# SyncE's queue asks for batch 1's q, k and v behind small reads of w_ch1's landed quarters

## Chip, cores and metric

The kernel runs on one core of one Trainium2 chip. The metric is the device time of one execution in microseconds (us). The profile's times count from the start of its span.

## The reference

Four batches, eight heads, 768 positions, head dimension 64. Attention with a window of 128 positions and 4 sink positions is followed by a residual MLP that mixes positions and then channels:

```python
scores = scale * q @ k^T             # kept where pos_k < 4 or 0 <= pos_q - pos_k < 128
x   = softmax(scores) @ v            # heads joined: (batch, 768, 512)
a1  = alpha1 * x + beta1
tok = einsum('ts,bsd->btd', w_tok, a1)
u   = x + lam * tok
a2  = alpha2 * u + beta2
out = u + lam * (relu(a2 @ w_ch1) @ w_ch2)     # w_ch1 512x2048, w_ch2 2048x512
```

Everything is given and returned in float32; the kernel multiplies in float16.

## The kernel before

One batch goes through these stages; the names are those of tiles in the profile.

- **Loads.** `nat` holds q or k of two heads (128x2x384 float32, 384 KB); a batch has eight of them, named by head pair and by q or k (`nat_1_0` is q of head pair 1). `load_qk` (L481) asks for them on SyncE's queue, but for six of batch 0 that GpSimd loads with a cast. `load_v` (L500) asks for `vnat`, six per batch, 256 KB each. `load_w` (L537) asks for `wst`, a staging tile with a pair of row blocks of w_ch2 (512 KB, eight in all). `load_w1` (L542) asks on GpSimd's queue, with a cast to float16, for `w1f`, a resident tile, in four quarters of 512 columns (512 KB each as written).
- **Transposes.** q and k are cast to `n` and turned by TensorE (`tp`, batches 0 and 1) or by DMA (batches 2 and 3) into `qkT`. The rows of w_tok are loaded to `wtn`, cast to `wt` and turned (`wT`) into `wtokT`.
- **Attention.** `S` holds scores, `sk` those of the sinks, `E` their exponentials, `pv` the products with v (cast to `vfs`), `x` the normalized result. VectorE normalizes (`rec` and `x`, L817 and L818), GpSimd multiplies by lam times alpha1 (`xh`), and VectorE adds the beta part (L841).
- **MLP.** `tok` multiplies `wtokT` with six `xh` tiles (six matmuls for each of six row tiles). VectorE adds it to `x`, `u` is the float16 copy, `uTp` its transposes in PSUM, `uT` the result of the affine step (two chunks of three row tiles each). `h` is the hidden layer: a unit is four matmuls for a chunk and one of 16 column blocks `fi` of w_ch1, and `h_0_5` is chunk 0, `fi` 5; it needs quarter `fi // 4` of `w1f`. Its relu is `hT`. `ch` multiplies it with `w2f`, which is w_ch2 times `lam_b`, made from `wst` by VectorE or GpSimd (L898), two products per `wst` tile.

The order on each engine is not written by hand. Every step is a task with a priority, a cost per engine and the tasks it needs; `Plan.run` (L130) plays the tasks through in advance and emits them in the order in which they then start. `Rings` (L35) models the two DMA queues there. `TURNS` is a list of seeds; each seed moves some priorities a little before the plan is made (`shuffle`, L262). Where TensorE would idle in the plan ahead of 36 us, matmuls on a zero tile are put in (`idle`, L342).

Buffers come in numbered homes: 8 for `nat`, 4 for `wst`, 4 for `vnat`, 12 for `x`, and 4 PSUM buffers `d` that `pv`, `tok`, `h`, `ch` and most transposes share. Two of the `wst` homes hold v of batch 0's second head group at first. An engine waits in its order: what stands behind a waiting instruction waits too. In the emitted program each DMA of SyncE's queue has one of eight semaphores in turn and waits for the transfer that had it before.

The tasks for the loads of batch 1 need nothing in the kernel before:

```python
for i, (hp, t) in enumerate(QK_ORDER):
    load_qk(t0 + 100 + i, 1, hp, t)
...
for r in range(NR):
    load_v(t0 + 300 + r, 1, r)
```

Of the kernel before, what the change touches and what calls it, by code (L numbers as in the profile page):

```python
# [10 lines left out]
FP16 = mybir.dt.float16  # L11
# [4 lines left out]
PE, ACT, DVE, POOL, SP = "pe", "act", "dve", "pool", "sp"  # L16
# [13 lines left out]


FW = 1.0


class Rings:  # L35
# [74 lines left out]
class Plan:  # L110
# [9 lines left out]
    def add(self, prio, engs, fn, after=(), uses=(), mode=None, lands=None, port=False,  # L120
            since=0.0):


        t = Task(len(self.tasks), prio, engs, fn, after, uses, mode, lands, port, since)
        for a in t.needs:
            a.then.append(t)
        self.tasks.append(t)
        return t

    def run(self, prio):  # L130
# [17 lines left out]
        rings = Rings()  # L148
# [3 lines left out]
        def end(t, seen):  # L152
            t.seen = seen
            for b in t.uses:
                b.left -= 1
                b.freed = max(b.freed, seen)
                if b.left == 0:
                    busy[b.kind][b.home] = False
                    homes[b.kind][b.home] = b.freed
            for o in t.then:  # L160
                ready[o.i] = max(ready[o.i], seen)
                waiting[o.i] -= 1
                if not waiting[o.i]:
                    bisect.insort(open_, (rank[o.i], o.i))
# [33 lines left out]
        while len(steps) < len(tasks):  # L198
            best = pick()
            if best is None or landing <= best[0]:  # L200
                assert landing < float("inf"), "no task can go on"
                t = rings.step(float("inf"))
                end(t, rings.now + 300.0)
                landing = rings.peek()
                continue
            start, r, _, i, e = best
            open_.pop(bisect.bisect_left(open_, (r, i)))
            t = tasks[i]
            for b in t.uses:
                if b.home is None:  # L210
                    b.home = min((h, n) for n, (h, x) in enumerate(zip(homes[b.kind], busy[b.kind]))
                                 if not x)[1]
                    busy[b.kind][b.home] = True
            idle = None
            n = int((start - max(free[PE], 400.0)) / (took if free[PE] > 4500.0 else 110.0))
            if e == PE and free[PE] < until and n > 0:
                spare = [(h, k) for k, (h, x) in enumerate(zip(homes["d"], busy["d"])) if not x]
                if spare and min(spare)[0] <= free[PE]:
                    idle = (min(spare)[1], n)
                    homes["d"][idle[0]] = start  # L220
                    mode = None
            cost = t.engs[e]
            if t.lands:
                cost += rings.room("sw" if e == POOL else "hw", t.lands, start) - start
            if e == PE:
                if start < 4500.0:
                    cost = cost * 2
                if t.mode != mode:
                    cost = cost + 95
                mode = t.mode  # L230
            free[e] = start + cost
            if e == POOL or (e == DVE and t.port):
                port = free[e]
            steps.append((t, e, start, free[e], idle))
            if t.lands:
                rings.step(start)
                rings.issue("sw" if e == POOL else "hw", t, free[e])
                landing = rings.peek()
            else:
                end(t, free[e] + SEEN[e])  # L240
# [34 lines left out]
def kernel(  # L275
# [123 lines left out]
    w1f = const.tile([P, NC, DFF], FP16, name="w1f")  # L399
    w2f = const.tile([P, NF, DM], FP16, name="w2f")  # L400

    ROWS = 7000.0

    PAIRS = 0

    TURNS = (39286, 39315, 39323, 39754, 40467, 41250, 41382, 139002, 39003, 39015, 139040, 139062, 139089, 139154, 39159, 139160, 39171, 39387, 139559, 139625, 139757, 139905, 39966, 140019, 140036, 140073)
    W1_SINCE = 20000.0

    V0 = (((0, 1), (2, 3), (4, 5)), ((0, 1, 2), (3, 4, 5)))
# [7 lines left out]
    done = {}  # L417
# [82 lines left out]
    def load_v(p, b, r, wait=None):  # L500
        bf = vn[b, r] = Buf("vnat", None, None, f"vnat{b}_{r}")
        done["vn", b, r] = add(
            p, {SP: 550}, lambda e: nc.sync.dma_start(
                bf.t, v[b, :, r * P : (r + 1) * P, :].rearrange("h p d -> p h d")),
            [wait], [bf], lands=(64, 19.0))
# [31 lines left out]
    def load_w(p, key, src):  # L537
        bf = wst[key] = Buf("wst", None, None, f"wst_{key}")
        done["wst", key] = add(
            p, {SP: 400}, lambda e: nc.sync.dma_start(bf.t, src), uses=[bf], lands=(16, 90))  # L540

    def load_w1(p, i):  # L542
        done["w1", i] = add(
            p, {POOL: 760}, lambda e: nc.gpsimd.dma_start(
                w1f[:, :, i * 512 : (i + 1) * 512],
                moe_w_ch1[:, i * 512 : (i + 1) * 512].rearrange("(c p) f -> p c f", p=P)),
            lands=(32, 96), since=W1_SINCE)

    def load_w2(p, i):
        for a in range(4 * i, 4 * i + 4, 2):  # L550
# [541 lines left out]
    load_w1(-770, 0)  # L1092
    for i in range(1, 4):
        load_w1(-769, i)

    def fold_rows():
        for name, key, o, p in (("a1", "la1", la1_b, -987), ("b1", "lb1b", lb1_b, -986)):
# [36 lines left out]
    for b in range(B):  # L1134
        w0 = STEP * b
        if b == 0:
            seq = [("tok", ti) for ti in range(3)] + [("uT", 0, 0), ("uT", 0, 1)]
            seq += [("tok", ti) for ti in range(3, NR)]
            m1 = []
            for qd in range(4):  # L1140
                for chk in range(2):
                    m1 += [("m1", chk, fi) for fi in range(4 * qd, 4 * qd + 4)]
            m1.insert(3, ("uT", 1, 0))
            m1.insert(5, ("uT", 1, 1))
        else:
            seq = [("tok", ti) for ti in range(NR)]
            m1 = [("m1", 0, fi) for fi in range(NF)]
            m1 += [("m1", 1, fi) for fi in range(NF)]
        seq += m1
        seq += [("m2", ti, part) for ti in range(NR) for part in range(4)]  # L1150
        ns = len(seq)
        if b == 0:
            for i, (hp, t) in enumerate(QK_ORDER):
                load_qk(t0 + 100 + i, 1, hp, t)
            done["lam"] = add(
                t0 + 150, {SP: 500}, lambda e: nc.sync.dma_start(
                    lam_b, moe_lam.unsqueeze(0).to_broadcast([P, DM])), lands=(8, 90))
            for i in range(4):
                load_w2(t0 + 200 + i, i)
                cast_w2(w0 + 22 + 4 * i, i)  # L1160
            for r in range(NR):
                load_v(t0 + 300 + r, 1, r)
        for i, (what, *args) in enumerate(seq):

            p = w0 + i - (LEAD if b and what == "tok" and args[0] < 3 else 0)
            {"tok": tok, "uT": uTp, "m1": mlp1, "m2": mlp2}[what](p, b, *args)
            if b and what == "tok":
                uTx(p + 0.3, b, *args)
        if b + 1 < B:
            nb = b + 1  # L1170
            if nb >= XB:
                for i, (hp, t) in enumerate(QK_ORDER):
                    load_qk(w0 + i, nb, hp, t, done["qkT", b, 3, 1])
                for r in range(NR):
                    load_v(w0 + 10 + r, nb, r, done["qkT", b, 3, 1])
            lo, hi = (1, ns - 14) if b else (LO, ns - 12)
            steps = [("T", i) for i in range(8)] + [("sk",)]
            for j in range(NR):
                steps += [("S", j)]
                steps += [("pv", j - 1, 0), ("pv", j - 1, 1)] if j else [("vs",)]  # L1180
            steps += [("pv", NR - 1, 0), ("pv", NR - 1, 1)]
            for r in range(NR):
                cast_v(w0 + lo + (hi - lo) * (r + 4) / len(steps), nb, r)
            for i, (what, *args) in enumerate(steps):
                p = w0 + lo + (hi - lo) * i / len(steps) + 0.5
                if what == "T":
                    hp, t = QK_ORDER[args[0]]
                    trans(p if nb < XB else w0 - 15 + i, nb, hp, t, {POOL: 829, ACT: 831}, {DVE: 955, ACT: 800},
                          wait=done["tok", b, 2])
                elif what == "sk":  # L1190
                    sinks(p, nb)
                elif what == "vs":
                    fill_vs(p, nb)
                elif what == "S":
                    j = args[0]
                    scores(p, nb, j, (0, 1) if j < NR - 1 else (None,))
                else:
                    pv(p, nb, *args)
# [37 lines left out]
```

The softmax here doesn't subtract the row's maximum and nothing guards it: scores larger than these inputs give would overflow.

## Time and profile before

| | |
|---|---|
| median of 6 runs | 262.83 us (262.21 to 263.61) |
| profiled execution, its own time | 263.61 us |
| its span | 261.9 us |
| TensorE matmul busy | 253.5 us, 97% |
| VectorE busy | 155.9 us, 60% |
| ScalarE busy | 134.2 us, 51% |
| GpSimd busy | 81.0 us, 31% |
| TensorE clock granted | full in all 40 slices |
| SyncE's DMA queue | 35.14 MB, 56.2% of 16 DMA engines |
| GpSimd's DMA queue | 3.28 MB, 7.7% |

The profiled execution is the slowest of the six. Busy time is the time in which an engine has an instruction in it; issuing of DMAs is not counted. SP is SyncE, PE is TensorE, DVE is VectorE, ACT is ScalarE and POOL is GpSimd.

### The profile page before, as it was taken

The page shows a single profiled execution, that of the slowest core. Times are in us where ns is not written, and L with a number is a line of the kernel's source. Part 1 is how long each engine was busy: PE and PEld are TensorE (multiplying, and loading weights), DVE is VectorE, ACT ScalarE, POOL GpSimd, SP SyncE. Part 2 cuts the span into 40 slices and gives each one's busy share as a digit, 9 for nine tenths or more (in the row PEclk, how much of TensorE's full clock was granted, in tenths as well). Part 3 has the DMA queues.
Part 4 walks back from the last instruction along what each step waited for, and adds up shares of the span by engine and source line. Part 5 has one row for each costly group of instructions (what it writes and reads, how often), then busy time and mean ns, then how long its engine had stood idle before and what let it go on. Part 6 is the DMA issues. An engine that isn't in the chain of part 4 may idle for free.

```text
span 261.9 us, 4960 instructions
## 1 busy us (share of the span) xinstructions
PE 253.5 (97%) x1954; PEld 139.8 (53%) x1954; DVE 155.9 (60%) x315; ACT 134.2 (51%) x219; POOL 81.0 (31%) x100
## 2 busy tenths in 40 slices
PE   7899989899999999999999999999999999999994
PEld 7554646465555544565555445556555445655453
DVE  4697994779999936755668534459965444000222
ACT  2788667479882224767741126788411136773000
POOL 8539951454711612143427203004223000000000
PEclk9999999999999999999999999999999999999999
DMA  7999999959936998899917669400012233000222
GB/s 177 195 244 373 297 290 279 299 132 316 216 82 168 238 200 186 176 219 217 174 50 170 167 128 228 84 0 3 0 41 83 68 92 83 0 0 3 81 80 80
DMA packets 85791, 38.76 MB, mean 148 GB/s; under 512 B 73460, under 2 KB 79868, under 8 KB 85768
## 3 DMA queue, kind: packets, MB, share of 16 engines
q1 hardware_dynamic: 81984, 35.14, 56.2%
q0 software_dynamic: 3744, 3.28, 7.7%
q8 instruction: 15, 0.25, 0.4%
q14 instruction: 8, 0.07, 0.1%
q10 hardware_dynamic: 40, 0.03, 0.0%
HBM read 29.91 MB, written 6.29 MB: 138 GB/s over the span
## 4 chain that ended last, share of the span: by engine, by line
PE 82%; DMA 11%; POOL 3%; DVE 2%; issue 0%; POOLq 0%
PE ch L1052 31%; PE h L996 28%; PE tok L916 9%; DMA w1f<-in_moe_w_ch_dram 7%; PE pv L792 4%; PE S L702 4%; DMA n<-in_k_dram 4%; PE S L697 1%; PE ch L1023 1%; POOL n L486 1%; POOL xh L827 1%; PE pv L785 1%; DVE x L841 1%; DVE E L731 1%; PE sk L639 1%; DVE x L818 0%
## 5 line engine op out<-in xcount | busy, mean ns | idle before, releaser
L996 PE MATMUL h<-uT,w1f 128*128 128x384 f16 x512 | 89.2, 326 | 1.5 <-DMA w1f<-in_moe_w_ch_dram 1.0
L1052 PE MATMUL ch<-w2f,hT 128*128 128x512 f16 x368 | 86.5, 379 | 0.1
L996 PEld LDWEIGHTS <-w1f 128*128 128x128 f16 x512 | 48.2, 98 | 34.8 <-issue 3.3
L1002 ACT ACTIVATE hT<-h 128x384 f16<-128x384 f32 x103 | 50.2, 491 | 25.2 <-PE h L996 24.6
L1052 PEld LDWEIGHTS <-hT 128*128 128x128 f16 x368 | 34.4, 98 | 38.1 <-issue 1.0
L722 ACT ACTIVATE E<-S 128x1024 f16<-128x1024 f32 (+1 forms) x42 | 40.6, 1003 | 12.2 <-PE S L702 10.6
L834 POOL TENSOR_TENSOR xh<-x,la_b 128x512 f16<-128x512 f32 x18 | 25.5, 1424 | 52.0 <-DVE x L818 36.2
L1063 DVE TENSOR_TENSOR x<-x,ch 128x512 f32<-128x512 f32 x23 | 15.8, 686 | 35.4 <-PE ch L1052 35.3
L916 PE MATMUL tok<-xh,wtokT 128*128 128x512 f16 x144 | 33.7, 379 | 0.0
L349 ACT CAST u<-x 128x512 f16<-128x512 f32 x17 | 10.5, 618 | 42.5 <-DVE x L923 42.5
L923 DVE TENSOR_TENSOR x<-x,tok 128x512 f32<-128x512 f32 x24 | 16.3, 686 | 19.8 <-PE tok L916 19.7
L841 DVE SCALAR_TENSOR_TENSOR x<-lb_b,rsum,x 128x512 f32<-128x512 f32 x24 | 22.1, 932 | 5.2 <-POOL xh L834 4.9
L1004 DVE TENSOR_SCALAR hT<-h 128x384 f16<-128x384 f32 x25 | 13.9, 555 | 16.6 <-PE h L996 16.2
L916 PEld LDWEIGHTS <-wtokT 128*128 128x128 f16 x144 | 14.0, 98 | 16.3
L818 DVE TENSOR_TENSOR x<-pv,rec 128x256 f32<-128x256 f32 x48 | 20.4, 425 | 1.7
L351 POOL CAST vfs<-vnat 128x512 f16<-128x512 f32 x18 | 12.7, 710 | 20.5 <-DMA vnat<-in_v_dram 12.9
L792 PEld LDWEIGHTS <-E 128*128 128x128 f16 x328 | 15.1, 97 | 6.4 <-issue 0.6
L731 DVE TENSOR_TENSOR E<-E,maskn 128x1024 f16<-128x1024 f16 x25 | 18.1, 745 | 0.0
L792 PE MATMUL pv<-vfs,E 128*128 128x65 f16 x328 | 17.8, 194 | 0.0
L351 POOL CAST u<-x 128x512 f16<-128x512 f32 x7 | 5.2, 742 | 37.1 <-DVE x L923 37.1
L351 POOL CAST n<-nat 128x768 f16<-128x768 f32 x12 | 10.1, 850 | 16.2 <-DMA nat<-in_q_dram 7.9
L349 ACT CAST n<-nat 128x768 f16<-128x768 f32 x12 | 9.9, 832 | 8.1 <-DMA nat<-in_k_dram 7.3
(99 smaller groups left out, 207.9 us busy)
## 6 DMA issues: line engine op xcount, KB each, us to landing
out_dram<-x SPq DMA_DIRECT2D x23, 256.0 KB, 2.4
nat<-in_q_dram SPq DMA_DIRECT2D x13, 384.0 KB, 5.4
nat<-in_k_dram SPq DMA_DIRECT2D x13, 384.0 KB, 7.2
vnat<-in_v_dram SPq DMA_DIRECT2D x18, 256.0 KB, 4.5
wst_w<-in_moe_w_ch_dram SPq DMA_DIRECT2D x8, 512.0 KB, 11.5
wtn<-in_moe_w_tok_dram SPq DMA_DIRECT2D x6, 384.0 KB, 5.5
w1f<-in_moe_w_ch_dram POOLq DMA_DIRECT2D x4, 512.0 KB, 15.6
v<-in_v_dram SPq DMA_DIRECT2D x12, 128.0 KB, 6.6
```

Of the source, the lines that this page charges most:

```text
L349: nc.scalar.copy(o, i)
L351: engine[e].tensor_copy(o, i)
L722: nc.scalar.activation(eT.t, pS.t[:, :, 0 : n * w].rearrange("p e (i w) -> p e i w", i=n), AF.Exp, scale=scale)
L731: nc.vector.tensor_mul(ev, ev, m.to_broadcast(list(ev.shape)))
L792: nc.tensor.matmul(po.t[:, hl, :], eT.t[:, e_, off + i, c : c + P], vf[j][:, h, :], start=(r < 2 and n == 0), stop=(n == len(parts) - 1 an ...
L818: nc.vector.tensor_mul(bx.t[:, 4 * G : 4 * G + 4, :], po.t[:, :, 0:D], rec.t.to_broadcast([P, 4, D]))
L834: engine[e].tensor_mul(bh.t, bx.t.rearrange("p h d -> p (h d)"), la1_b)
L841: engine[e].scalar_tensor_tensor(out=xf, in0=lb1_b, scalar=rsum[:, r : r + 1], in1=xf, op0=ALU.mult, op1=ALU.add)
L916: nc.tensor.matmul(pt.t, wtokT[:, si, ti * P : (ti + 1) * P], hs[si].t, start=(si == 0), stop=(si == NR - 1))
L996: nc.tensor.matmul(ph.t, w1f[:, c, fi * P : (fi + 1) * P], bu.t[:, c, chk * NTOK : (chk + 1) * NTOK], start=(c == 0), stop=(c == NC - 1))
L1002: nc.scalar.activation(bh.t[:, fi, :], ph.t, AF.Relu)
L1052: nc.tensor.matmul(pc.t, bh.t[:, fi, nt * P : (nt + 1) * P], w2f[:, fi, :], start=(fi == 0), stop=(fi == NF - 1))
```

## The change

A small tile `gates` is added. `gate(i)` is a DMA on SyncE's queue that reads eight elements of quarter `i` of `w1f` in SBUF into `gates`; as it reads the quarter, the program makes it wait for the quarter's landing. `GATES = (-1, 2, 3)` sets which landing the tasks of three groups of loads wait for in the plan: w_ch2's none, batch 1's q and k that of quarter 2, batch 1's v that of quarter 3. The plan now takes a GpSimd transfer for landed 1800 ns after its last byte in the model instead of 300 (`SWDONE`). The list `TURNS` is another one, so the order of all engines differs through the whole program; SyncE's order is given in the prediction as far as it matters.

```diff
+SWDONE = 1800.0
...
-                end(t, rings.now + 300.0)
+                end(t, rings.now + (SWDONE if POOL in t.engs else 300.0))
...
+    gates = const.tile([1, 32], FP16, name="gates")
+
+    GATES = (-1, 2, 3)
...
-    TURNS = (39286, 39315, 39323, ... 26 seeds)
+    TURNS = (176180, 41742, 158411, ... 21 seeds)
...
     def load_w(p, key, src):
-            p, {SP: 400}, lambda e: nc.sync.dma_start(bf.t, src), uses=[bf], lands=(16, 90))
+            p, {SP: 400}, lambda e: nc.sync.dma_start(bf.t, src), [done.get(("w1", GATES[0]))], uses=[bf], lands=(16, 90))
...
+    def gate(i):
+
+        add(-3000, {SP: 420}, lambda e: nc.sync.dma_start(
+            gates[0:1, 8 * i : 8 * i + 8], w1f[0:1, 0, i * 512 : i * 512 + 8]), [done["w1", i]],
+            lands=(1, 20))
...
+    for i in sorted(set(GATES)):
+        if i < 0:
+            continue
+        gate(i)
...
-                load_qk(t0 + 100 + i, 1, hp, t)
+                load_qk(t0 + 100 + i, 1, hp, t, done.get(("w1", GATES[1])))
...
-                load_v(t0 + 300 + r, 1, r)
+                load_v(t0 + 300 + r, 1, r, done.get(("w1", GATES[2])))
```

## The prediction

> **What bounds the kernel now.** I read the busy shares first, then windows cut at the places where TensorE stops, then its order of time, the chain of waits and SyncE's queue.
>
> ```profile
> PE 253.5 (97%) x1954; PEld 139.8 (53%) x1954; DVE 155.9 (60%) x315; ACT 134.2 (51%) x219; POOL 81.0 (31%) x100
> ```
> TensorE is the bound. The windows (length, then busy time per engine; clock, DMA share and GB/s at the end) say where it is not full:
>
> ```profile
> 34.82:38.48 3.66, 2.67 (x38) 2.15 (x37) 3.56 (x6) 3.44 (x5) 2.67 (x4) 1.00 1.12 293
> 38.48:50.70 12.22, 10.90 (x76) 6.29 (x77) 7.05 (x13) 7.63 (x15) 3.02 (x5) 1.00 1.13 296
> 50.70:60.00 9.30, 9.30 (x74) 5.81 (x76) 7.20 (x12) 6.51 (x14) 6.61 (x7) 1.00 0.65 158
> 60.00:92.00 32.00, 32.00 (x270) 17.29 (x267) 29.98 (x56) 19.31 (x27) 12.67 (x10) 1.00 0.88 205
> 92.00:258.60 166.60, 166.51 (x1110) 88.64 (x1108) 80.88 (x158) 75.69 (x130) 31.68 (x34) 1.00 0.47 100
> ```
> From 50.70 to the end nothing is left to win; only the stretch before it has holes. TensorE's order of time there:
>
> ```profile
> 34.82 1.69 PE L597 MATMUL tp<-iden,n 128*128 128x128 f16 x18
> 37.16 0.84 PE L957 MATMUL uTp<-iden,u 128*128 128x128 f16 x12 [0.64 <-POOL u L351]
> 39.11 1.46 PE L996 MATMUL h<-uT,w1f 128*128 128x384 f16 x7 [0.32 <-DVE uT L942]
> 46.95 2.75 PE L916 MATMUL tok<-xh,wtokT 128*128 128x512 f16 x12
> 50.70 0.50 PE L996 MATMUL h<-uT,w1f 128*128 128x384 f16 x2 [1.00 <-DMA w1f<-in_moe_w_ch_dram]
> ```
> Per group of the chain of waits TensorE needs 0.65 us for four h matmuls (one "unit"), 1.29 for six tok, 0.34 for six transposes. Between 34.82 and 50.70 stand 6 groups of transposes of batch 1 (2.0), 2 of uTp (0.7), 2 of wT (0.7), 10 h units (6.5) and 12 tok matmuls (2.6): 12.45 us of work in 15.88, so **3.4 us are lost**, 1.96 of them as bracketed waits. The last is for a quarter of w1f:
>
> ```profile
> 31.04 19.62 DMA w1f<-in_moe_w_ch_dram
> 50.70 2.12 PE h L996 x12
> ```
> The four quarters, issued by GpSimd at 23.42, 24.23, 28.84 and 31.04, land 10.6, 15.4, 15.7 and 19.6 us later: about 34.0, 39.6, 44.5 and 50.7, over 5 us apart. In that time SyncE's queue is full:
>
> ```profile
> 30.03 1.65 SPq L1156 DMA_DIRECT2D lam_b<-in_moe_lam_dram  x1
> 32.57 5.36 SPq L540 DMA_DIRECT2D wst_w<-in_moe_w_ch_dram  x3
> 39.13 9.40 SPq L503 DMA_DIRECT2D vnat<-in_v_dram  x2
> ```
> Two issues take 9.4 us because, in the program's list, every SyncE transfer waits for the landing of the one eight places earlier.
>
> **What the Trainium skill says.** "DMA: Bandwidth & Descriptors", section "Queues, rings and completion order": each DMA engine goes round-robin over the rows that have work, packet by packet. So w1f's row gets more when SyncE's is empty. The trace agrees as far as it goes: 5 us per 512 KB quarter with both rows full at 293 to 296 GB/s. The same page, "Anatomy of one DMA — SWDGE (gpsimd) path": a semaphore wait is served on the issuing sequencer. So a read that waits for a quarter holds all behind it in SyncE's order; the 9.4 us above show such holding. "Perfetto Trace Analysis", "Tensor Engine Instruction (MATMUL, LD_WEIGHTS)": the end of a matmul is estimated. Agreed: 18 transposes show 1.69 us "busy" for 1.01 of work, so I count starts, not busy time.
>
> **The change, part by part.** Both instruction lists side by side show three things.
>
> (a) SyncE's order. Before, eight q and k loads of batch 1 (384 KB each) stand between and behind the w_tok loads, issued 19.3 to 29.3. After, it is: v and w_tok of batch 0, seven of the eight w2 loads and lam, gate 2, eight q/k, the last w2, gate 3, six v. 3.1 MB of q and k and 0.5 MB of v leave the stretch in which w1f travels; its w2 loads come earlier. Till w1f is complete there are then from 21 us: 1.6 MB w_tok, 2.1 w2, 0.26 lam, 2.1 w1f, 6.1 MB in all, at 290 GB/s 21 us: the last quarter by about 42, not 50.7; the third by 40. Bounds: 37 (the 373 GB/s of the best slice) and 50 (no gain).
>
> (b) TensorE's order. Work is the same but for 97 fillers for 88, nine of 0.065: 0.6 us, all but one ahead of tok. All six tok run before h; h begins with quarter 0; batch 1's transposes move behind h_0_8, h_1_7 and h_0_9 (quarter 2). Before, 207.9 us pass from h_0_0 (50.70) to the last matmul (258.62). After, the 6 groups of transposes and 10 units that before stand ahead of h_0_0 stand behind it: 2.0 + 6.5. So **the end = start of h_0_0 + 216.4**, if nothing stalls later; equal time at 42.2.
>
> When does h_0_0 start? VectorE's order now puts the casts wt_0, wt_1, wt_2 ahead of x_4 and of the second head group. wt_0 waits for the first w_tok landing: 16.58 + 5.2 = 21.8 before, one place earlier now, say 21.3. Then wt 3 x 0.87, six normalizations x 0.55, vs 0.34 and one wtokT copy 0.5 give x_3 at 28.1; GpSimd's xh of it (0.7) ends between 28.8 and, behind the earlier ones, 29.7. I take tok_0 at 29.3 (29.24 before), with five wT done instead of three. From tok_0 to h_0_0 lie 36 tok x 0.2157, one wT, two uTp: 8.8 us. But VectorE still has two x, three wtokT, five beta steps (0.74 to 1.02) and the adds (0.62) to do; u_2 is cast by 38.0 to 38.4 and TensorE is at uTp by 37.5: 0.5 to 0.9 lost. After uTp the four affine steps (0.67 on ScalarE, 0.43 on VectorE) have no transposes of batch 1 to cover them any more: 1.3. h_0_0 at 29.3 + 8.8 + 2.3 = 40.4, so the end at 256.8: **1.8 us less**.
>
> (c) The gates. Two issues of 0.4 us on SyncE's queue, hidden. The trace shows no such tiny transfer; landing between 1.7 us (the shortest of all, a 128 KB output) and the page's fixed cost of about 2; only the transfer eight places on waits for it: nothing. The wait itself: the w2 load ahead of gate 2 needs a staging buffer that VectorE frees with w2_2's second product, behind h_0_2's relu, about 43.6. So gate 2 is reached at 44.1, after quarter 2: wait 0, at worst 0.4 beyond a landing at 44.5. Behind it wait the eight loads: issued from 44.5, first landed at 48 to 49 (4 us, the shortest of their kind), then 1.2 us each (384 KB at 300), eighth by 57; GpSimd's casts 0.85 each, done at 58. TensorE asks for the first at 52.8 (18 units and two uTp after 40.4), for the last at 60.3 (seven more groups with seven units between, 0.99 each, and a unit extra): cover of 2.3 us. The v loads land from 60 on, first wanted at 63.5. If that cover is gone, each further us of delay costs one us.
>
> (d) The planner's SWDONE and new TURNS only change the order of the later batches; at tok, h and ch of batches 1 to 3 both lists keep the same distances within 1 us, so I take 0, with -0.3 and +0.8 as ends.
>
> Sum: -1.8 against the profiled execution (span 261.9, last matmul 258.62, own time 263.61; median of six 262.83). From the median: **261.0**.
>
> **Rivals.** *Early chain eats it*: if w_tok lands 1 to 2 us later than 21.3, or the four PSUM buffers hold pv behind x_4, tok_0 moves one for one and h_0_0 comes at 41.4 to 42.9: 262.0 to 263.5. For it: VectorE is 12.95 of 15 us busy in 14 to 29. Against: in the order before it also waits till 22.6 for its first wt. *Larger gain*: the affine and uTp holes are half as large and tok_0 comes at 28.3 since five wT are done: 259.0. *Loads too late (slower)*: SyncE's order makes q/k wait for gate 2 and for VectorE's w2 products. With the eighth cast at 58 for 60.3, it begins to cost when the loads begin at 46.8, it outweighs the gain of 1.8 beyond 48.6, and at 51 it gives 265.2. TensorE's order is fixed, so nothing else slips in between. For it: VectorE's 5 w2 products took 4.58 us beside GpSimd, 0.92 each instead of 0.69. Against: 2.3 us of cover. *The gates do nothing*: the queue reaches them after the landings and the move is all in the order; the time is the forecast's.
>
> **How the numbers follow.** Forecast with the larger gain 0.63; early chain 0.18 (mostly within the bound); loads too late or a stall in the later batches 0.19. A measurement tells about 0.3%, 0.8 us, from no change: faster below 262.0, slower above 263.6. The likeliest alone spans 259.0 to 262.0; the range to 264.2 takes in the early chain and half of the late loads.
>
> **What would show it.** Right: w1f's landings 10 to 13 us after issue, the last by 43; no wait of TensorE for w1f; SyncE at gate 2 at 43 to 45; holes only around uTp, 2 us; h_0_0 at 40 to 41 and solid after. Wrong: h_0_0 after 42.2; a wait of tp or of its cast on nat; holes after 62.

## The result, and the profile after

| | before | changed |
|---|---|---|
| median | 263.14 us (262.21 to 264.35, 73 runs) | 264.32 us (262.46 to 266.59, 36 runs) |
| ratio to before | | 1.0044 (95%: 1.0032 to 1.0055) |
| profiled execution, its own time | 263.61 us | 263.59 us |
| its span | 261.9 us | 261.9 us |

The change makes the kernel slower by 0.44%, 1.2 us. The forecast was 261.0, faster. The two profiled executions are alike in time, which hides that most executions of the changed kernel (26 of 36) are slower than this one; they spread over 4 us where the old ones spread over 2.

First TensorE's order of time after the change (start, length, engine, line, what, shape, count, and in brackets the wait ahead of it):

```profile
29.53 1.03 PE L927 MATMUL tok<-xh,wtokT 128*128 128x512 f16 x4
...
31.65 6.32 PE L927 MATMUL tok<-xh,wtokT 128*128 128x512 f16 x28
38.04 0.27 PE L968 MATMUL uTp<-iden,u 128*128 128x128 f16 x2
38.70 0.73 PE L968 MATMUL uTp<-iden,u 128*128 128x128 f16 x10 [0.38 <-ACT u L351]
40.05 0.32 PE L1007 MATMUL h<-uT,w1f 128*128 128x384 f16 x1 [0.62 <-DVE uT L953]
40.98 4.93 PE L1007 MATMUL h<-uT,w1f 128*128 128x384 f16 x19 [0.61 <-ACT uT L951]
```

The wait for `w1f` is gone, all `tok` come ahead of `h`, and `h_0_0` starts at 40.05 (forecast 40.4). After 41 no wait is left. But the last row has 19 matmuls in 4.93 us, 0.26 each, where 0.16 each is usual (0.65 for four). The windows (length, busy time of PE, PEld, DVE, ACT and POOL, granted TensorE clock, DMA share, GB/s) show why:

```profile
41.00:42.00 1.00, 1.00 (x5) 0.53 (x5) 1.00 (x2) 0.16 (x1) 0.77 (x1) 0.66 1.13 292
42.00:43.00 1.00, 1.00 (x5) 0.50 (x4) 0.02 (x1) 0.33 (x1) 0.56 (x1) 0.50 1.18 253
43.00:44.00 1.00, 1.00 (x5) 0.48 (x4) 0.00 (x0) 0.88 (x2) 0.00 (x0) 0.50 1.23 213
44.00:45.00 1.00, 1.00 (x6) 0.47 (x4) 0.60 (x2) 0.12 (x1) 0.97 (x1) 0.63 1.19 283
45.00:46.00 1.00, 1.00 (x11) 0.68 (x10) 1.00 (x2) 0.55 (x2) 0.29 (x1) 1.00 0.89 328
46.00:92.00 46.00, 46.00 (x397) 26.57 (x395) 38.86 (x69) 27.57 (x45) 19.82 (x20) 1.00 0.81 214
```

TensorE is "busy" all the time from 41 to 45, but at half clock: 5 or 6 matmuls fall into a microsecond, where the same work at full clock shows 8 (the run without gates below, 43 to 45 us). Adding up what the granted clock leaves out from 41 to 45 gives 0.34 + 0.50 + 0.50 + 0.37 = 1.7 us. The last matmul ends at 258.3; the forecast's 216.4 from `h_0_0` and these 1.7 give 40.05 + 216.4 + 1.7 = 258.15.

This is one of two losses. The other doesn't show in this execution, and is found below.

### The profile page after: what moved, and what is told of

Read it like the earlier page. It is cut to its first block, busy times and chain, and to the rows that moved or that the text cites. A ratio compares the mean times of both kernels' runs of the same rounds, so it can differ in the third digit from the quotient of the medians.

```text
span 261.9 us, 4953 instructions
## 1 busy us (share of the span) xinstructions
PE 254.2 (97%) x1963; PEld 140.5 (54%) x1963; DVE 153.6 (59%) x315; ACT 132.7 (51%) x219; POOL 82.4 (31%) x100
## 4 chain that ended last, share of the span: by engine, by line
PE 83%; DMA 10%; SPq 4%; DVE 1%; POOL 1%; issue 0%; ACT 0%; POOLq 0%; ACTq 0%
PE h L1007 33%; PE ch L1063 30%; PE tok L927 9%; DMA wst_w<-in_moe_w_ch_dram 6%; SPq L525 3%; PE pv L803 3%; PE S L713 3%; DMA lam_r<-in_moe_lam_dram 2%; DMA v<-in_v_dram 2%; PE ch L1034 1%; PE tp L608 1%; PE pv L796 1%; PE pv L700 0%; PE sk L650 0%; SPq L536 0%
## 5 line engine op out<-in xcount | busy, mean ns | idle before, releaser
L1007 PE MATMUL h<-uT,w1f 128*128 128x384 f16 x512 | 90.5, 330 | 1.2 <-DVE uT L953 0.6
L1063 PE MATMUL ch<-w2f,hT 128*128 128x512 f16 x368 | 85.6, 379 | 0.0
L1013 ACT ACTIVATE hT<-h 128x384 f16<-128x384 f32 x105 | 51.5, 491 | 24.9 <-PE h L1007 24.5
L845 POOL TENSOR_TENSOR xh<-x,la_b 128x512 f16<-128x512 f32 x18 | 26.6, 1483 | 56.5 <-DVE x L829 52.6
L351 ACT CAST u<-x 128x512 f16<-128x512 f32 x21 | 12.9, 617 | 45.5 <-DVE x L934 45.5
L852 DVE SCALAR_TENSOR_TENSOR x<-lb_b,rsum,x 128x512 f32<-128x512 f32 x24 | 23.5, 994 | 1.8 <-POOL xh L845 1.7
L934 DVE TENSOR_TENSOR x<-x,tok 128x512 f32<-128x512 f32 x24 | 16.2, 684 | 11.9 <-PE tok L927 11.8
L1015 DVE TENSOR_SCALAR hT<-h 128x384 f16<-128x384 f32 x23 | 12.7, 554 | 14.9 <-PE h L1007 14.8
L353 POOL CAST vfs<-vnat 128x512 f16<-128x512 f32 x18 | 11.9, 661 | 23.4 <-DMA vnat<-in_v_dram 18.6
L353 POOL CAST n<-nat 128x768 f16<-128x768 f32 x14 | 12.0, 859 | 16.7 <-DMA nat<-in_q_dram 9.7
L353 DVE COPY qkT<-tp 128x768 f16<-128x768 f16 x11 | 10.4, 955 | 5.4 <-PE tp L608 4.6
L713 PE MATMUL S<-qkT 64*128 64x256 f16 (+1 forms) x168 | 13.4, 269 | 0.0
```

What stands on the lines that cost most here:

```text
L353: engine[e].tensor_copy(o, i)
L713: nc.tensor.matmul(pv_[:, e_, i, :], o.t[rows, 2 * hp + 1, j * P : (j + 1) * P], o.t[rows, 2 * hp, j * P : j * P + w], start=not bias, sto ...
L845: engine[e].tensor_mul(bh.t, bx.t.rearrange("p h d -> p (h d)"), la1_b)
L852: engine[e].scalar_tensor_tensor(out=xf, in0=lb1_b, scalar=rsum[:, r : r + 1], in1=xf, op0=ALU.mult, op1=ALU.add)
L1007: nc.tensor.matmul(ph.t, w1f[:, c, fi * P : (fi + 1) * P], bu.t[:, c, chk * NTOK : (chk + 1) * NTOK], start=(c == 0), stop=(c == NC - 1))
L1013: nc.scalar.activation(bh.t[:, fi, :], ph.t, AF.Relu)
```

## The experiments

Five theories appear in the expectations. **A**: the clock falls to half after the holes around 38 to 41 us. **B**: data of batch 1 come late. **C**: the later batches' new order is slower. **D**: GpSimd's products `w2f` (`wst_w` times `lam_b`), which now come at 31 to 38 us, hold VectorE's beta steps `x<-lb_b,rsum,x`. **E**: VectorE has simply too much to do at the end of the attention. A run's ratio is to runs of the kernel before on the same chip; their medians were 263.06 to 263.37.

### The changed kernel again

Nothing edited, timed anew with another profile, and one more single execution.

> The changed kernel once more, for a second profile and for the granted clock of every run. Theory A (clock): TensorE half-idles from 38.0 to 41.0 us, the granted clock falls to half for some 3 us in a part of the runs, and each such run loses about 1.7 us; the runs with a mean clock of 1.000 are then at or below the kernel before (262.5 or less), those at 0.994 about 1.7 us above them. Theory B (late data): a wait for a transfer that this first profile does not show, in the attention of batch 1, costs 1 to 2 us in most runs; then runs with a clock of 1.000 too are above the kernel before, and the profile shows idle time of TensorE after 54 us. Theory C (later batches): the new order of batches 2 and 3 loses steadily; then the last stretch from 103 us on is longer than the 155.4 us of the kernel before.

> A third profile of the changed kernel. Theory A: whether its time is above or below 263 goes with whether the clock falls at 41 to 45 us. Theory B: TensorE waits after 54 us. Theory C: the stretch from batch 1's first h at 103 us to the last matmul is above 155.4 us.

Measured: 263.91 us (263.05 to 266.29, 15 runs), ratio 1.0039 (1.0016 to 1.0063); the single one 265.72. The records split by clock: in the first set of the changed kernel 13 of 37 executions show a mean clock of 0.994 or less (13 times 263.6 to 266.6), here 5 of 15 (median 265.8); the others are at 0.997 or more, with medians of about 263.9 and 263.4. The kernel before was never under 0.998 in 31. Theory A expected 262.5 or less at full clock, so the clock is not the whole loss. TensorE's waits in this second profile (who waits, for whom, us in total, times, longest):

```profile
PE tok L927 <- DVE x L934: 1.5, 1, 1.5
PE h L1007 <- DVE uT L953: 0.6, 1, 0.6
PE h L1007 <- ACT uT L951: 0.6, 1, 0.6
PE uTp L968 <- ACT u L351: 0.4, 1, 0.4
PE uTp L968 <- DVE x L934: 0.2, 1, 0.2
```

The first row is not in the first profile. It is `tok_2`, which needs a PSUM buffer that VectorE frees with the add of an earlier `tok`. `h_0_0` starts at 41.57, though the first `tok` was at 29.28, earlier than in the first profile. No wait after 43.4 exists in any of the three profiles, so B falls; from batch 1's first `h` to the last matmul they take 155.2 us each (155.6 before), so C falls.

Why is VectorE late? Its order of time, then GpSimd's at the same place:

```profile
30.68 0.56 DVE L353 COPY wtokT<-wT 128x768 f16<-128x768 f16 x1 [0.57 <-PE wT L887]
31.15 3.50 DVE L852 SCALAR_TENSOR_TENSOR x<-lb_b,rsum,x 128x512 f32<-128x512 f32 x1
```

```profile
30.92 0.74 POOL L838 TENSOR_TENSOR xh<-x,la_b 128x256 f16<-128x256 f32 x1
31.61 2.49 POOL L909 TENSOR_TENSOR w2f<-wst_w,lam_b 128x512 f16<-128x512 f32 x2
```

**One beta step takes 3.50 us**; its usual time is 0.74 (the median of the six is 741 ns, the longest 3505). It ends at 34.65, 0.55 after GpSimd's second product. So it stood, counted as busy, until GpSimd was through `xh` and both products. The add `x<-x,tok`, whose other operand lies in PSUM, takes 673 ns in every case. In the first profile `lam_b` landed later, the products started at 33.12 instead of 31.61, and the first three beta steps slipped in ahead of them:

```profile
31.40 2.41 DVE L852 SCALAR_TENSOR_TENSOR x<-lb_b,rsum,x 128x512 f32<-128x512 f32 x3
34.93 2.47 DVE L852 SCALAR_TENSOR_TENSOR x<-lb_b,rsum,x 128x512 f32<-128x512 f32 x2
```

Of the later two, one took 1.80 us and again ended 0.55 after the second product. That execution was a lucky one, but not free of the hold. In the third profile the hold was split: the first two steps took 1.84 and 1.75 us, each ended 0.54 to 0.55 after one of the two products, and the second product took 1.72 us instead of 1.27. In the kernel before, GpSimd's products came after this chain, the next one at 59.21:

```profile
51.47 2.93 POOL L898 TENSOR_TENSOR w2f<-wst_w,lam_b 128x512 f16<-128x512 f32 x2
```

`lam_b` was issued at 30.03 there, behind q and k, and at 22.07 in the first profile of the changed kernel.

"SBUF — State Buffer", section "Who interferes with whom", of the Trainium skill says that a VectorE instruction with two SBUF inputs contends with a GpSimd instruction that reads SBUF, and that the loser blocks fully. The 3.50 us agree with it, and so does the add with one operand in PSUM. That a step can be held over two products in a row, and not over one only, is read from this trace.

### TensorE filled ahead of h_0_0

```diff
         def mm(e):
+            if (b, chk, fi) == (0, 0, 0):
+                idle(ph.t, 24)
             for c in range(NC):
```

> 24 matmuls on the zero tile are put ahead of h_0_0's own four, into its PSUM tile, which h_0_0 then overwrites: 24 x 0.056 = 1.3 us of work in the hole of 39.4 to 41.0, nothing else moved. Theory A: the clock stays at 1.000 in all runs and the mean falls by the share of throttled runs times 1.7 us, 0.5 to 0.8 us below the changed kernel. Theories B and C: no change within 0.3 us, but for up to 0.3 us more where the fillers end after the affine step.

Measured: 264.63 us (263.61 to 265.54, 7 runs), ratio 1.0060 (1.0040 to 1.0081), clock 0.998 or more in all seven. No execution was throttled. At the changed kernel's rate (18 of 52) seven in a row would come out so by chance once in twenty, so this run alone supports A's first half only weakly; the clock windows in the last section say more. The fillers don't bring the time down: they start at 41.97 and `h_0_0` follows at 43.31, so they fill the hole and run on past it, and `tok_2` still waits 1.51. The throttle is a second loss, not the first.

### Without the gates

```diff
-        add(-3000, {SP: 420}, lambda e: nc.sync.dma_start(
-            gates[0:1, 8 * i : 8 * i + 8], w1f[0:1, 0, i * 512 : i * 512 + 8]), [done["w1", i]],
-            lands=(1, 20))
+        add(-3000, {SP: 420}, lambda e: None, [done["w1", i]], lands=(1, 20))
```

> The two gates are planned as before but nothing is emitted for them; every engine keeps the order of the changed kernel. In the changed kernel's profile gate 2 is issued at 46.34 and the next load at 47.17, 0.4 us more than between two loads, and gate 3 stands between 52.8 and 53.8. If the gates' waits cost anything (part of theory B), this kernel is faster than the changed one by 0.5 to 1 us, and its v of batch 1 lands 1 us earlier. By theories A and C it is the same within 0.3 us.

Measured: 265.23 us (263.30 to 267.40, 16 runs), ratio 1.0071 (1.0046 to 1.0095), clock 0.994 or less in 8 of 16. Its profile has full clock, `tok_2` waiting 1.38, a first beta step of 3.27 us, `h_0_0` at 41.20 and the last matmul's end at 257.75: the same hold without any throttle. Removing the gates doesn't remove the loss. No theory had this kernel slower than the changed one; more throttled executions are a part of it, but those above 0.994 are slower too (median 264.3 for 263.4), and why stays open. How much the gates do themselves is taken up in the last run.

### Small products on GpSimd

GpSimd multiplies 64 of 512 columns and writes zeros to the rest:

```diff
+    def product(e, a, src):
+        n = 64 if e == POOL else DM
+        if n < DM:
+            nc.gpsimd.memset(w2f[:, a, n:], 0.0)
+        engine[e].tensor_mul(w2f[:, a, :n], src.t[:, a % 2, :n], lam_b[:, :n])
```

> Leaves out most of what GpSimd multiplies: each of its five products w2f = wst_w x lam_b works on 64 of 512 columns, and the other columns of those five blocks are set to zero by a GpSimd memset ahead of it; the order of all engines is that of the changed kernel. Theory D (GpSimd's first two products hold the beta step that VectorE has at the same time: 3.5 us instead of 0.74 where lam has landed by 31 us): every beta step of 30 to 40 us at 0.74 to 0.9, no wait of TensorE for tok_2, second part of h_0_0 at 40.0 to 41.2 in every profile, clock full or nearly always, median 262.0 to 262.7. Theory E (VectorE is late at the end of the attention because it has too much work there, with wt ahead of x; the products are beside the point): wait for tok_2 stays at 1.0 to 1.5, median 263.9 as the changed kernel.

Measured: 262.03 us (261.29 to 263.40, 6 runs), ratio 0.9957 (0.9933 to 0.9981), clock 0.997 or more in all. The first three beta steps take 2.54 us together, `tok_2` doesn't wait, and `h_0_0` is at 40.32, 10.0 behind the first `tok` (12.3 in the second profile of the changed kernel). Against 1.0039 that is 0.8%, some 2.2 us: the held step with the throttle that follows it. E falls, since VectorE's work is the same.

### The beta step moved, in three ways

With one operand in PSUM, in the changed kernel and in the one before:

```diff
+            if b == 0:
+                nc.vector.scalar_tensor_tensor(
+                    out=pt.t, in0=lb1_b, scalar=rsum[:, ti : ti + 1], in1=pt.t, op0=ALU.mult, op1=ALU.add)
             nc.vector.tensor_add(xf, xf, pt.t)
```

> Batch 0's beta step is taken from where it stood (operands x and lb_b, both in SBUF) and done directly ahead of the add of tok on the tok buffer in PSUM (tok = lb_b x rsum + tok, one operand in SBUF); work and order otherwise as in the changed kernel. Theory D: a step with one SBUF operand isn't held by GpSimd's products, as the add with tok (0.67 in all profiles) isn't: 0.65 to 0.75 each beside them, u_2 ready by 36.5, no wait for tok_2 over 0.3 us, second part of h_0_0 at 40.0 to 41.5, median 262.0 to 262.9. Theory E: VectorE has as much to do as ever, now all of it behind tok: wait for tok_2 1.0 or more, uTp 0.7 later, 263.9 to 264.7.

> The same move of batch 0's beta step in the kernel before. There the first three beta steps took 3.06 us instead of 2.2, but the start of the last stretch without holes is set by w1f's third and fourth quarters landing at 44.5 and 50.7. Theory D and E alike: no change, 262.9 to 263.5. If the beta step matters there too: below 262.5.

Measured: 265.75 us (265.68 to 266.20, 5 runs), ratio 1.0101 (1.0084 to 1.0118), and 265.38 (265.10 to 265.74, 6 runs), ratio 1.0084 (1.0069 to 1.0100). Both expectations were wrong on the time. On the hold D was right: beside the same two products (31.57, 2.49 us) the step takes

```profile
32.08 0.75 DVE L937 SCALAR_TENSOR_TENSOR tok<-lb_b,rsum,tok 128x512 f32<-128x512 f32 x1 [0.83 <-PE tok L929]
```

and `tok_2` doesn't wait. But the step now can't start before `tok` is there. VectorE stands idle 0.83 and 1.31 us for it, then has the step and the add of two more row tiles to do ahead of the affine step, for which TensorE waits:

```profile
41.62 0.48 PE L1012 MATMUL h<-uT,w1f 128*128 128x384 f16 x1 [1.67 <-DVE uT L958]
```

In the kernel before, TensorE got new holes of 0.34, 0.96 and 0.89 us at 35 to 38. All 11 executions of the two show a lowered clock.

The order of VectorE's steps alone, and the order together with later products:

```diff
+    plan.moves = [(xb(4), u(2)), (xb(5), xb(4))]
```

```diff
+        if e == POOL and a in (12, 13):
+            r = a - 11
+            nc.gpsimd.tensor_copy(behind[:, r : r + 1], x[0, r].t[0:1, 0, 0:1])
...
+    plan.moves = [(w(12), xb(1)), (w(13), xb(2)), (xb(4), u(2)), (xb(5), xb(4))]
```

`(s, t)` in `moves` puts step s directly behind t in the emitted list; `xb` are beta steps, `u` adds, `w` products.

> The order of the beta steps alone: x_4 and x_5 behind the add of tok_2, GpSimd's products left where they were. Theory D: the first beta step, now of x_0, is still held to about 3.5 us by the last xh and the two products where lam has landed by 31; one beta step less stands ahead of the add that tok_2 waits for, so the wait is 0.8 to 1.0 instead of 1.5, median 263.0 to 263.9. If the order of VectorE's steps is the whole loss: as the run with both, 261.4 to 262.5.

> Complete kernel: the changed one, with batch 0's beta steps of x_4 and x_5 put behind the add of tok_2 on VectorE, and GpSimd's first two w2f products each put behind a one-element copy that reads x_1 and x_2, so they start when the beta steps of x_1 and x_2 are done and run beside the adds with tok. Theory D: beta steps of x_0, x_1, x_2 take 0.74 each, or up to 0.5 more beside the last xh; no wait of TensorE for tok_2 over 0.3; second part of h_0_0 at 40.0 to 41.3 (10.9 behind the first tok, as in the run with small products); clock full in nearly all runs; median 261.4 to 262.5. Theory E (amount of work on VectorE): the work is the same, so tok_2 still waits over 1 us and the median is 263.9. A rival on the other side: the later products free wst later, SyncE's w2 loads and the gate slip by 2 us, and batch 1's transposes wait: 264 to 266 with waits of tp between 52 and 62.

Measured: 265.39 us (263.77 to 266.07, 6 runs), ratio 1.0075 (1.0050 to 1.0099), and 265.65 (262.66 to 268.00, 18 runs), ratio 1.0062 (1.0039 to 1.0084). The wait of `tok_2` is gone in both. In the first kernel the first beta step wasn't held for the expected 3.5 us: the first two took 1.08 and 1.75. But another wait took the place of the old one; in the second kernel it is

```profile
40.66 0.49 PE L983 MATMUL uTp<-iden,u 128*128 128x128 f16 x6 [1.67 <-DVE x L949]
```

The add of `tok_5`, which frees the PSUM buffer that this `uTp` takes, stands behind the beta step of x_5, and that had been moved back. In 14 of the second kernel's 18 executions the clock was lowered. This was a mistake in the edit, not in D; the next one leaves VectorE's order alone.

### Only the products moved

```diff
+            r = 1 if a == 12 else 5
+            nc.gpsimd.tensor_copy(behind[:, a - 12 : a - 11], x[0, r].t[0:1, 0, 0:1])
...
+    plan.moves = [(w(12), xb(1)), (w(13), xb(5))]
```

> Complete kernel: the changed one with VectorE's order as it is there; GpSimd's first w2f product is put behind a one-element copy that reads x_1 after its beta step, the second behind one that reads x_5 after its step, so both run beside adds with tok. Theory D: the first five beta steps take 0.74 each (the first up to 1.2 beside the last xh, the fourth up to 1.1), tok_2 and the second uTp wait less than 0.4 us, second part of h_0_0 10.9 to 11.4 behind the first tok (it was 11.5 to 13.2 in the four profiles of the changed order), clock full or nearly always, median 261.8 to 262.7. Rival (a buffer is what counts: the first run of this kind, with the beta steps of x_4 and x_5 put later, lost its gain to a tok buffer held for the add of x_5): no, since the order is the old one. Rival on the other side: w2 loads and gate slip 2 us, tp waits between 52 and 62: 264 to 266.

> The same with ten fillers of TensorE ahead of h_0_0's own matmuls, which fit in the hole of 0.6 to 0.7 us before it. Theory A (after a stretch with holes the granted clock drops to half for 3 us in part of the executions): clock 0.997 or more in all of them, so the median is that of the run without fillers where that has no throttled execution, and up to 1.0 lower where half of its executions are throttled: 261.8 to 262.7. If fillers cost their own time: 0.6 more.

Measured: **261.95 us** (261.07 to 262.99, 6 runs), ratio 0.9938 (0.9918 to 0.9958), and with ten fillers 261.83 (261.02 to 262.92, 7 runs), ratio 0.9942 (0.9921 to 0.9962). Nothing is left out in either, and both beat the kernel before and the changed one. The clock is 0.999 or more in all 13. GpSimd's order of time and the six beta steps in the first of them:

```profile
35.06 0.18 POOL L916 COPY behind<-x 1x1 f32<-1x1 f32 x1 [1.95 <-DVE x L861]
35.20 1.27 POOL L917 TENSOR_TENSOR w2f<-wst_w,lam_b 128x512 f16<-128x512 f32 x1
37.75 0.17 POOL L916 COPY behind<-x 1x1 f32<-1x1 f32 x1 [1.28 <-DVE x L861]
```

```profile
L861 DVE SCALAR_TENSOR_TENSOR x<-lb_b,rsum,x x6: 739/824/1083, 32.6 to 40.6; 128x512 f32<-128x512 f32 x6
```

The products wait 1.95 and 1.28 us and TensorE waits for none of them; the longest beta step (minimum, median, maximum in ns) is 1083 instead of 3505. (In the kernel with fillers the sixth step is held to 2.16 us beside a later product; TensorE doesn't wait for it.) VectorE's order and work are those of the changed kernel, so E falls here too. In TensorE's order of time

```profile
32.83 6.32 PE L942 MATMUL tok<-xh,wtokT 128*128 128x512 f16 x28
40.70 0.32 PE L1022 MATMUL h<-uT,w1f 128*128 128x384 f16 x1 [0.68 <-DVE uT L968]
41.63 3.25 PE L1022 MATMUL h<-uT,w1f 128*128 128x384 f16 x19 [0.61 <-ACT uT L966]
```

only the two waits of the affine step are left, and the 19 matmuls take 3.25 us instead of 4.93. The fillers show no gain beyond this, as there was no throttle left to prevent.

### The parts of the change

The gates, `GATES` and `SWDONE` with the old seeds in `TURNS`, and the good kernel without gates:

```diff
-    TURNS = (176180, 41742, 158411, ... 21 seeds)
+    TURNS = (39286, 39315, 39323, ... 26 seeds)
```

> One part of the change alone: gates, GATES and SWDONE as changed, with the seeds of the kernel before in TURNS, so the plan's order is another one everywhere. If the gates and the later landing in the model bring the gain or loss by themselves: about the changed kernel's 263.9, with w1f's last quarter by 48. If the list of seeds carries it: the old seeds were not made for this plan, 264.5 to 268, with waits of TensorE spread over the stretches after 60 us.

> The complete kernel with GpSimd's products put apart, without the gates themselves (their two small reads are not issued; the order of all else stays). The first run without gates had 265.23 against 263.91, with a throttled clock in half of its executions against a third, so what the gates do by themselves is not told from it. If they do nothing (SyncE reaches them behind the landings they wait for): 261.8 to 262.3, h_0_0 at 10.0 behind the first tok, q and k loads 0.8 us earlier or as early, no wait of TensorE after 46. If they hold back loads that otherwise slow w1f or w2: later h_0_0 or a wait for w1f, 262.8 or more.

Measured: 267.81 us (266.21 to 268.31, 4 runs), ratio 1.0166 (1.0136 to 1.0195), with `uTp` waiting 2.03 us at 41.04: the list of seeds matters more than the gates. And 262.29 us (261.40 to 264.05, 19 runs), ratio 0.9968 (0.9952 to 0.9983), no wait of TensorE after 46, `h_0_0` 10.0 behind the first `tok`. Without the gates the kernel still beats the one before. Whether they bring the last tenths can't be said: the two intervals, 0.9918 to 0.9958 and 0.9952 to 0.9983, just touch. The first pair, 1.0039 with gates and 1.0071 without, points the same way, and its intervals overlap.

## Why the prediction was wrong

The gain foreseen was there: with the hold gone the ratio is 0.9938, and the forecast's 261.0 against its 262.83 was 0.9930. That these two agree so well is in part luck: in the four profiles without the hold the first `tok` came at 29.26 to 30.71, mostly later than the 29.3 of the forecast, and the way from it to `h_0_0` took 9.9 to 10.0 us instead of 11.1. Point by point:

- **(a) SyncE's order, landings.** The order was as told. The landings were not: the quarters of `w1f`, issued at 21.59, 24.34, 26.11 and 30.36, took 11.8, 14.4, 18.0 and 17.3 us, not 10 to 13, so the last came at 47.7 instead of 42. It cost nothing, as TensorE waited for none of them. Why the sum of bytes came out short was not tried. One candidate is in the sum itself: it takes `w1f` at its 2.1 MB as written, but the transfer reads float32, twice that. With 2.1 MB more at the same 290 GB/s the estimate would be about 49.
- **(b) The end is the start of h_0_0 plus 216.4.** Right: 216.5 in the profiles at full clock (41.20 to 257.75 without gates, 40.32 to 256.86 with small products).
- **(b) The start of h_0_0.** The first `tok` was forecast at 29.3 and came at 29.26 to 30.71. From there to `h_0_0` the forecast had 8.8 of work and 2.3 of holes, 11.1. Measured with the hold: 12.3, 11.9 and 12.2 in three profiles, and 10.5 in the lucky one; without it 10.0. **The step that failed** is "five beta steps (0.74 to 1.02)": behind GpSimd the first took 3.27 to 3.51 us in three profiles with this order, and in a fourth the first two took 1.84 and 1.75. The 1.02 was the mean of three steps from before (1.17, 1.30 and 0.74), where GpSimd had no product in that place; the change itself brought the products there, by bringing `lam` and `w2` early. The text even had the right row, VectorE's products stretched from 0.69 to 0.92 beside GpSimd, and used it for the gates instead.
- **The clock.** The prediction has no term for it. A throttled execution loses 1.4 to 1.7 us, and a third of those of the changed kernel were throttled. In the four kernels where the hold was taken away and no other wait took its place, none of 38 executions was under 0.996; in the three where another wait did take its place, 23 of 29 were at 0.994 or less. So the throttle goes with the holes, whatever makes them.
- **(c) The gates.** Gate 2 at 46.34 for 44.1, the loads from 47.17 for 44.5, the eighth cast done at 60.0 for 58, the last group of transposes at 62.41 for 60.3: all 2 to 3 us late, so the cover of 2.4 us is near the forecast's 2.3 because both of its ends moved alike. No wait, as forecast; the slower rival, loads too late, did not happen.
- **(d) Later batches.** 0 was taken; by the constant of (b) it is 0.1.
- **The rivals.** "Early chain eats it" had the right place, the chain ahead of `h_0_0`, and a wrong cause, `w_tok` or `pv`. Its 262.0 to 263.5 lacks the throttle. What made the kernel slower was on none of the lists.

## What to carry to other kernels

Ask of a transfer that is made to come earlier which computation it sets free, on which engine, and what that engine shares with the one on the critical path; here the data came earlier by design and the products that they released stopped VectorE. An instruction that counts as busy may be waiting: compare the longest of a group with its median before trusting a mean. Take a second profile when the runs spread, since the first may be the lucky execution. And look at how much idle time falls together, not only at the longest hole: small holes close to each other can cost a second time, through the clock.

## What the runs showed of the hardware

- A VectorE step on two SBUF operands (0.74 us alone) was held by GpSimd's `xh` and products, and the time counted as busy. In seven profiles the held steps ended 0.54 to 0.56 us after the end of the GpSimd instruction that they stood behind. In three of them the step got no turn between two products (3.27 to 3.51 us); in two it did (1.84 and 1.75; 1.08 and 1.75), and there the second product took 1.72 us instead of 1.27. What decides between the two is open. With one operand in PSUM the step took 0.75 beside the same products.
- The granted clock was set window by window. In the clock records of all 15 traces it changes only at whole multiples of 3.41 us after its first rise to full, which lies 3.8 to 6.9 us into the span. Seven of the eight throttled profiles have one such window at half clock, and the eighth, of the changed kernel with the step on PSUM, has two in a row. Here are three windows of the changed kernel's second profile, then three of the kernel without gates (length, TensorE's busy time, other engines, clock):

```profile
35.87:39.29 3.42, 2.66 (x12) 1.17 (x12) 3.42 (x6) 1.22 (x2) 1.27 (x1) 1.00 1.17 261
39.29:42.70 3.41, 1.62 (x16) 0.94 (x15) 3.41 (x7) 2.45 (x4) 1.74 (x2) 1.00 1.20 238
42.70:46.11 3.41, 3.41 (x12) 1.59 (x11) 1.80 (x3) 1.49 (x3) 2.27 (x2) 0.50 0.52 95
33.40:36.81 3.41, 2.03 (x10) 0.81 (x9) 3.41 (x5) 0.44 (x1) 1.22 (x2) 1.00 1.16 274
36.81:40.23 3.42, 2.99 (x20) 1.46 (x19) 3.42 (x6) 1.84 (x4) 0.52 (x1) 1.00 1.14 274
40.23:43.64 3.41, 2.18 (x18) 1.25 (x16) 3.41 (x6) 2.06 (x5) 3.05 (x3) 1.00 1.06 182
```

- Up to 250 us, nine windows in the eight throttled profiles had TensorE busy for 1.82 us or less, and each was followed by half clock; no window with 1.88 or more was, in any of the 15. The two profiles above have nearly the same holes, 3.3 and 3.0 us, and differ in how the windows cut them. The first profile of the changed kernel was throttled with no single hole over 0.62 us: three of 0.38, 0.62 and 0.61 lay in one window, with 1.72 busy. Where only the products were moved, the two waits that are left add up to 1.29 us, which leaves about 2.1 busy even if both fall into one window. Busy time isn't the exact measure: just ahead of the end, windows with 1.59 to 1.72 busy were followed by full clock.
- "TensorE: Matmul & The Clock Gate", section "What's actually happening", of the Trainium skill says that the clock follows how busy TensorE was in a window of 3413 ns that runs freely and doesn't reset when the kernel starts. The 3.41 us and the scattered first rises agree with it, and it would explain why only a part of a kernel's executions is throttled.
